# Attention with a fused projection: who copies the o banks, and how the two query casts share a PSUM tile

## Chip, cores, metric

One core of one Trainium2 chip. The metric is the device time of one execution in microseconds (us); for one core that is also the time of the slowest core.

## The reference, cut to what matters

```python
xn = _layernorm(x)                                   # x: 1 x 2048 x 640, bf16
q  = (xn @ wq).reshape(B, Sq, 32, 192)               # 32 heads of 192
p  = softmax(q @ k_cache^T * 192**-0.5)              # 2048 keys for each head
s  = (p @ v_cache) @ wo
g  = silu(swiglu_ffn(xn))                            # 640 -> 1536 -> 640
return x + s * g
```

(The two products are written here as `@`; the reference has them as einsums.) All inputs are bf16. Attention dominates: 32 heads, 2048 queries, 2048 keys.

## The kernel before: the parts that matter

Attention is a stream of 32 x 4 x 8 = 1024 *pairs* (head, block of 512 queries, pair of key tiles). Eight pairs are a *block*; there are 128. At the head of each block (for the first block, inside it) TensorE also computes a query projection of the next head (20 matmuls of 512 columns), so that the queries are there before TensorE needs them; in the last head, two products of the FFN take its place.

```python
def two_products(W, qs):
    ps = ps_st.tile([P, 1024], F32, tag="st2", name="ps")      # the same two buffers as the scores
    ...                                                        # 20 matmuls into two banks
    return ps

def cast_pair(qAB, ps):                                        # PSUM fp32 -> SBUF bf16
    nc.vector.tensor_copy(out=qAB[:, 0, :], in_=ps[:, 0:512])
    nc.scalar.copy(out=qAB[:, 1, :], in_=ps[:, 512:1024])

def emit_scores(h, qb, p):
    st2 = ps_st.tile([P, 1024], F32, tag="st2", name="st2")    # two buffers of two banks each
    ...                                                        # six matmuls
    nc.scalar.activation(out=pT2[:], in_=st2[:], func=ACT.Exp, scale=att_scale)

def values(n):
    ...                                                        # 16 matmuls into obanks[0] and obanks[1]
    if p < NPAIR - 1: return
    nc.scalar.copy(out=osum[:], in_=ov[0])                     # the o copy, once in a block
    nc.vector.tensor_tensor(out=osum[:], in0=osum[:], in1=ov[1], op=ALU.add)

for n, (h, qb, p) in enumerate(stream):
    if p == 0 and n > 0: project(h + 1, qb)                    # two_products, cast_pair, moves by DMA
    scores(n + 2)
    values(n)
    if p == 0 and n > 0: finish_block(n - 1)
    ...                                                        # first head: layernorm of later rows too
```

Terms: a *cast* here is a copy of one half of the projection's result `ps` from PSUM (fp32) to SBUF (bf16); the *o banks* are the two PSUM accumulators of a block's attention output; the *o copy* moves the first of them to `osum`, and the add after it adds the second.

The tag `st2` has two buffers, used in turn: scores of pair n+1, projection, scores n+2, scores n+3. So scores n+3, the *second* scores after a projection, write the buffer that the projection's `ps` held, and must wait until both casts have read it.

## Time and profile before

| | before |
|---|---|
| time | 1989.2 us, median of 3 runs (1988.92 to 1989.59) |
| TensorE (PE) busy | 1958.4 us, 99% |
| ScalarE (ACT) busy | 1260.5 us, 63% |
| VectorE (DVE) busy | 530.7 us, 27% |
| start to start of two projections | 12.933 us in a regular block |

The page of the kernel before: its span, the busy line of section 1 (us, share of the span, number of instructions), and section 4, the chain of work that ended last.

```profile
span 1987.2 us, 60137 instructions
...
PE 1958.4 (99%) x27351; PEld 1395.6 (70%) x27351; DVE 530.7 (27%) x861; ACT 1260.5 (63%) x1405; POOL 319.2 (16%) x572
...
PE 88%; DVE 5%; ACT 4%; issue 1%; DMA 1%; ACTq 0%; DVEq 0%
PE obank L446 30%; PE st L417 27%; PE ps L359 13%; PE ps_s L106 10%; DVE qAB L364 4%; ACT qAB L365 4%; PE st L418 3%; PE ps_f L612 3%; PE ps_gu L586 1%; DMA vt<-in_A_k_cache_dram 1%; PE ps L340 0%; ACT pT L420 0%; DVE stats L295 0%; PE pk L
```

PE seems full, yet the chain goes through both casts (L364 and L365) for 8% of the span. The table of waits of the kernel before (who waited for whom: us in total, times, longest):

```profile
ACT qAB L365 <- DVE qAB L364: 223.5, 126, 1.9
...
PEld L418 <- issue: 35.5, 131, 0.8
```

ScalarE's cast waits for VectorE's cast once in a block (126 times). On the side of PE the loss appears almost only at the weight loads (PEld), and without a culprit ("issue"); the table of PE itself names ScalarE's cast for 1.0 us in 4 waits. One such place in the timeline of the kernel before (start, duration, engine, line, operation, and in brackets the idle time before it and what ended it):

```profile
999.76 0.38 PE L417 MATMUL st<-qAB,KA 64*128 64x512 bf16 x1
...
999.97 0.69 DVE L364 CAST qAB<-ps 128x512 bf16<-128x512 f32 x1
...
1000.40 0.85 PE L446 MATMUL obank<-vt,pT 64*128 64x193 bf16 x16
...
1000.70 0.58 ACT L365 CAST qAB<-ps 128x512 bf16<-128x512 f32 x1 [1.77 <-DVE qAB L364]
...
1001.34 0.37 PE L417 MATMUL st<-qAB,KA 64*128 64x512 bf16 x1
1001.34 0.09 PEld L418 LDWEIGHTS <-KA 64*128 64x128 bf16 x1 [0.26 <-issue]
```

The first scores after the projection start at 999.76, the second at 1001.34, that is 1.58 us later, where the other pairs of a regular block follow one another by 1.314 (by 3.47 where the projection lies between). The values matmuls (L446) are modelled to end at 1001.25, so the PE row shows almost no gap; it is the distance between starts that tells. The second scores start 0.06 us after ScalarE's cast ends at 1001.28.

### The profile page before, as it was taken

The page shows a single profiled execution, that of the slowest core. Times are in us where ns is not written, and L with a number is a line of the kernel's source. Part 1 is how long each engine was busy: PE and PEld are TensorE (multiplying, and loading weights), DVE is VectorE, ACT ScalarE, POOL GpSimd, SP SyncE. Part 2 cuts the span into 40 slices and gives each one's busy share as a digit, 9 for nine tenths or more (in the row PEclk, how much of TensorE's full clock was granted, in tenths as well). Part 3 has the DMA queues.
Part 4 walks back from the last instruction along what each step waited for, and adds up shares of the span by engine and source line. Part 5 has one row for each costly group of instructions (what it writes and reads, how often), then busy time and mean ns, then how long its engine had stood idle before and what let it go on. Part 6 is the DMA issues. An engine that isn't in the chain of part 4 may idle for free.

```text
span 1987.2 us, 60137 instructions
## 1 busy us (share of the span) xinstructions
PE 1958.4 (99%) x27351; PEld 1395.6 (70%) x27351; DVE 530.7 (27%) x861; ACT 1260.5 (63%) x1405; POOL 319.2 (16%) x572
## 2 busy tenths in 40 slices
PE   7999999999999999999999999999999999999999
PEld 5677777777777777777777777777777777577776
DVE  5422222222222222222222222222222223521111
ACT  4677777777777777777777777777777777310000
POOL 3211111111111111111111111111111110000000
PEclk9999999999999999999999999999999999999999
DMA  7423232324332434363433333332323240838873
GB/s 179 90 55 93 58 90 62 97 62 95 67 98 67 98 67 95 67 158 67 98 67 96 65 98 67 80 83 56 92 54 92 59 98 3 232 63 153 153 148 60
DMA packets 362022, 177.96 MB, mean 90 GB/s; under 512 B 305712, under 2 KB 348976, under 8 KB 361760
## 3 DMA queue, kind: packets, MB, share of 16 engines
q1 hardware_dynamic: 334512, 116.21, 27.4%
q0 software_dynamic: 22736, 54.43, 11.1%
q8 instruction: 216, 3.54, 0.7%
q10 hardware_dynamic: 4512, 3.41, 0.6%
q14 instruction: 46, 0.38, 0.1%
HBM read 52.82 MB, written 27.79 MB: 41 GB/s over the span
## 4 chain that ended last, share of the span: by engine, by line
PE 88%; DVE 5%; ACT 4%; issue 1%; DMA 1%; ACTq 0%; DVEq 0%
PE obank L446 30%; PE st L417 27%; PE ps L359 13%; PE ps_s L106 10%; DVE qAB L364 4%; ACT qAB L365 4%; PE st L418 3%; PE ps_f L612 3%; PE ps_gu L586 1%; DMA vt<-in_A_k_cache_dram 1%; PE ps L340 0%; ACT pT L420 0%; DVE stats L295 0%; PE pk L255 0%; PE pst L311 0%
## 5 line engine op out<-in xcount | busy, mean ns | idle before, releaser
L420 ACT ACTIVATE pT<-st 128x1024 bf16<-128x1024 f32 x1024 | 1047.0, 1023 | 209.0 <-PE st L418 203.2
L446 PEld LDWEIGHTS <-pT 64*128 64x128 bf16 x16384 | 745.8, 94 | 208.2 <-issue 0.4
L446 PE MATMUL obank<-vt,pT 64*128 64x193 bf16 x16384 | 867.1, 243 | 0.0
L417 PE MATMUL st<-qAB,KA 64*128 64x512 bf16 x1024 | 384.7, 376 | 13.2 <-ACT qAB L365 1.0
L418 PE MATMUL st<-qAB,KA 64*128 64x512 bf16 x1024 | 386.6, 378 | 0.0
L417 PE MATMUL st<-qC,KC 64*128 64x512 bf16 x1024 | 384.8, 376 | 0.8 <-DVE KC L264 0.8
L417 PE MATMUL st<-qC,KB 64*128 64x512 bf16 x1024 | 384.7, 376 | 0.8 <-DMA qC<-qAB 0.6
L418 PE MATMUL st<-qAB,KB 64*128 64x512 bf16 x1024 | 385.1, 376 | 0.0
L418 PE MATMUL st<-qC,KC 64*128 64x512 bf16 x1024 | 385.1, 376 | 0.0
L456 DVE TENSOR_TENSOR osum<-osum,obank 128x772 f32<-128x772 f32 x128 | 122.6, 958 | 945.8 <-ACT osum L455 945.8
L329 POOL DMA_DIRECT2D qC<-qAB x254 | 133.9, 527 | 1286.5 <-DVE rl_all L462 1265.4
L359 PE MATMUL ps<-xnT,W 64*128 64x512 bf16 x1280 | 299.5, 376 | 0.0
L359 PE MATMUL ps<-xnS,W 64*128 64x512 bf16 x1280 | 293.7, 376 | 0.0
L365 ACT CAST qAB<-ps 128x512 bf16<-128x512 f32 x128 | 74.9, 585 | 227.0 <-DVE qAB L364 223.5
L359 PEld LDWEIGHTS <-W 64*128 64x128 bf16 x2560 | 143.4, 94 | 103.4 <-issue 0.2
L106 PE MATMUL ps_s<-wo_sb,oT 128*128 128x256 bf16 (+3 forms) x1536 | 208.8, 299 | 0.0
L106 PEld LDWEIGHTS <-oT 128*128 128x128 bf16 x1536 | 148.3, 98 | 60.5
L417 PEld LDWEIGHTS <-KC 64*128 64x128 bf16 x1024 | 96.0, 94 | 105.0 <-DVE KC L264 1.1
L463 DVE TENSOR_TENSOR ostage<-osum,rl_all 128x768 bf16<-128x768 f32 x128 | 122.6, 957 | 4.4
L418 PEld LDWEIGHTS <-KA 64*128 64x128 bf16 x1024 | 96.1, 94 | 34.4 <-issue 33.9
L417 PEld LDWEIGHTS <-KA 64*128 64x128 bf16 x1024 | 96.3, 94 | 15.6 <-issue 1.3
L417 PEld LDWEIGHTS <-KB 64*128 64x128 bf16 x1024 | 96.1, 94 | 12.9
(76 smaller groups left out, 1035.2 us busy)
## 6 DMA issues: line engine op xcount, KB each, us to landing
vt<-in_A_v_cache_dram SPq DMA_DIRECT2D x32, 768.0 KB, 6.5
o_scr<-ostage SPq DMA_DIRECT2D x16, 1536.0 KB, 9.3
qC<-qAB POOLq DMA_DIRECT2D x381, 64.0 KB, 2.0
wo_sb<-in_A_wo_dram POOLq DMA_DIRECT2D x1, 7680.0 KB, 37.9
W<-in_A_wq_dram POOLq DMA_DIRECT2D x32, 160.0 KB, 3.3
KC<-KA POOLq DMA_DIRECT2D x31, 128.0 KB, 5.2
KC<-KB POOLq DMA_DIRECT2D x31, 128.0 KB, 5.3
x_all<-in_A_x_dram SPq DMA_DIRECT2D x4, 640.0 KB, 9.7
```

The lines of the kernel that those rows point to most:

```text
L106: nc.tensor.matmul(ps[:, 0:w], lhsT=oT[:, k, :], rhs=wo_sb[:, k, c0:c1], start=(k == 0), stop=(k == OC - 1))
L329: nc.gpsimd.dma_start(out=qC[0:64, half, :], in_=qAB[64:P, half, :])
L359: nc.tensor.matmul(ps[:, r * 512:(r + 1) * 512], lhsT=W[rows, j, :], rhs=xs[rows, j // 2, qs], start=(j == 0), stop=(j == 2 * DC - 1))
L364: nc.vector.tensor_copy(out=qAB[:, 0, :], in_=ps[:, 0:512])
L365: nc.scalar.copy(out=qAB[:, 1, :], in_=ps[:, 512:1024])
L417: nc.tensor.matmul(st2[:, 0:512], lhsT=k0, rhs=q0, start=r == 0, stop=r == 2)
L418: nc.tensor.matmul(st2[:, 512:1024], lhsT=k1, rhs=q1, start=r == 0, stop=r == 2)
L420: nc.scalar.activation(out=pT2[:], in_=st2[:], func=ACT.Exp, scale=att_scale)
L446: nc.tensor.matmul(obanks[r][:, j * 256:j * 256 + DH + 1], lhsT=pT2[r * 64:(r + 1) * 64, t * 512 + j * P:t * 512 + (j + 1) * P], rhs=vt[r ...
L456: nc.vector.tensor_tensor(out=osum[:], in0=osum[:], in1=ov[1], op=ALU.add)
L463: nc.vector.tensor_tensor(out=ostage[:, qb * 4:qb * 4 + 4, hg * DH:(hg + 1) * DH], in0=osum[:, :, 0:DH], in1=rl.unsqueeze(2).to_broadcast( ...
L612: nc.tensor.matmul(ps[:, b * 512:b * 512 + c1 - c0], lhsT=hT[:, fc, i * P:(i + 1) * P], rhs=w2_sb[:, fc, c0:c1], start=(fc == 0), stop=(fc ...
```

## The change

Its intent: take the o copy off ScalarE, give each query half a tile of its own, and let the two casts run at once. The diff, cut to its core:

```diff
-            qtiles[h, qb] = (qp.tile([P, 2, 512], BF16, tag="qAB", name="qAB"), qlp.tile(...))
+            qtiles[h, qb] = ([qp.tile([P, 512], BF16, tag=t, name=t) for t in ("qA", "qB")],
+                             qlp.tile(...))
 ...
     def cast_pair(qAB, ps):
-        nc.vector.tensor_copy(out=qAB[:, 0, :], in_=ps[:, 0:512])
-        nc.scalar.copy(out=qAB[:, 1, :], in_=ps[:, 512:1024])
+        a = nc.vector.tensor_copy(out=qAB[0][:], in_=ps[:, 0:512])
+        b = nc.scalar.copy(out=qAB[1][:], in_=ps[:, 512:1024])
+
+        tc.declare_no_dep(b.ins, a.ins, reason="two banks, two destinations")
 ...                       # every use of qAB[:, half, :] becomes qAB[half][:]
-        nc.scalar.copy(out=osum[:], in_=ov[0])
+        nc.vector.tensor_copy(out=osum[:], in_=ov[0])
```

`declare_no_dep` tells the scheduler that the second cast need not be ordered after the first.

More of the change, by code (lines that the diff above doesn't have):

```diff
@@ L324, in q_tiles @@
         if (h, qb) not in qtiles:
-            qtiles[h, qb] = (qp.tile([P, 2, 512], BF16, tag="qAB", name="qAB"), qlp.tile([P, 2, 512], BF16, tag="qC", name="qC"))
+            qtiles[h, qb] = ([qp.tile([P, 512], BF16, tag=t, name=t) for t in ("qA", "qB")],
+                             qlp.tile([P, 2, 512], BF16, tag="qC", name="qC"))
         return qtiles[h, qb]
     def move_q(qAB, qC, half):
-        nc.gpsimd.dma_start(out=qC[0:64, half, :], in_=qAB[64:P, half, :])
+        nc.gpsimd.dma_start(out=qC[0:64, half, :], in_=qAB[half][64:P, :])
         if half == 0:
-            nc.gpsimd.dma_start(out=qC[64:P, 0, :], in_=qAB[0:64, 0, :])
+            nc.gpsimd.dma_start(out=qC[64:P, 0, :], in_=qAB[0][0:64, :])
     def project0(qb, half):
@@ L342, in project0 @@
         copy = nc.scalar.copy if half else nc.vector.tensor_copy
-        copy(out=qAB[:, half, :], in_=ps[:, 0:512])
+        copy(out=qAB[half][:], in_=ps[:, 0:512])
         if qb > 0:
@@ L375, in ffn_open @@
     def ffn_open(qb):
-        pairs[qb] = qp.tile([P, 2, 512], BF16, tag="qAB", name="qAB")
+        pairs[qb] = [qp.tile([P, 512], BF16, tag=t, name=t) for t in ("qA", "qB")]
         cast_pair(pairs[qb], two_products(wrest["wf"], slice(qb * 512, (qb + 1) * 512)))
@@ L382, in ffn_close @@
         t = hbp.tile([P, 512], BF16, tag="pt", name="pt")
-        nc.scalar.activation(out=t[:], in_=z[:, 0, :], func=ACT.Tanh, scale=0.5)
-        nc.vector.scalar_tensor_tensor(out=t[:], in0=t[:], scalar=1.0, in1=z[:, 0, :], op0=ALU.add, op1=ALU.mult)
+        nc.scalar.activation(out=t[:], in_=z[0][:], func=ACT.Tanh, scale=0.5)
+        nc.vector.scalar_tensor_tensor(out=t[:], in0=t[:], scalar=1.0, in1=z[0][:], op0=ALU.add, op1=ALU.mult)
         nc.vector.scalar_tensor_tensor(out=hT[:, FCP, qb * 512:(qb + 1) * 512], in0=t[:], scalar=0.5,
-                                       in1=z[:, 1, :], op0=ALU.mult, op1=ALU.mult)
+                                       in1=z[1][:], op0=ALU.mult, op1=ALU.mult)
     def swiglu(h, qb):
@@ L391, in swiglu @@
         qs = slice(qb * 512, (qb + 1) * 512)
-        z = qtiles[h, qb][0][0:PGW, 1, :]
+        z = qtiles[h, qb][0][1][0:PGW, :]
         r0 = (m % 2) * PGW
@@ L412, in emit_scores @@
         st2 = ps_st.tile([P, 1024], F32, tag="st2", name="st2")
-        rounds = [(KA[0:64, lo], qAB[0:64, 0, :], KA[64:P, hi], qAB[64:P, 0, :]),
-                  (KB[0:64, lo], qC[0:64, 0, :], KB[64:P, hi], qAB[64:P, 1, :]),
+        rounds = [(KA[0:64, lo], qAB[0][0:64, :], KA[64:P, hi], qAB[0][64:P, :]),
+                  (KB[0:64, lo], qC[0:64, 0, :], KB[64:P, hi], qAB[1][64:P, :]),
                   (KC[0:64, lo], qC[0:64, 1, :], KC[64:P, lo], qC[64:P, 0, :])]
```

## The prediction

> **What bounds it now.** TensorE: the page gives PE 1958.4 us busy of 1987.2 (99%), ScalarE 63%, VectorE 27%. Attention runs to about 1697 us as 128 blocks of eight pairs (scores, exponential, values), each with one projection at its head. In the timeline around 1000 us the score matmuls of two pairs start 1.314 us apart (3.47 with the projection between). One interval per block differs: the scores of the second pair after the projection start 1.579 us after the ones before (999.76 to 1001.34), 0.265 us late. Over the matmul starts of the whole trace this happens in 121 of 128 blocks; block to block is 12.933 us where 12.67 would do. Pipelined matmuls drain over the gap, so PE shows only 13.2 us idle at this line; the table of waits shows it at the weight loads, 35.5 us in 131 waits, put down to "issue".
>
> **Its cause.** These scores reuse the PSUM buffer of the projection's `ps`, which both casts must leave. VectorE's cast runs 999.97 to 1000.66 and only then ScalarE's, 1000.70 to 1001.28, though ScalarE had been idle since 998.93 (table of waits: 223.5 us in 126 waits for VectorE's cast). PE resumes at 1001.34. The chain of waits runs through the casts (4% + 4%), although PE was held for only 0.265 us of each 1.3.
>
> **What the change does.**
> - Casts side by side, in tiles of their own: `ps` is free after the longer one, at about 1000.67 instead of 1001.28. PE wants it at 999.76 + 1.314 = 1001.07. So the wait goes whole, with 0.35 us to spare; what the casts gain beyond 0.265 us is worth nothing.
> - o copy from ScalarE (0.797 us) to VectorE. Estimate 0.96 us: VectorE's 512-element fp32 cast takes 0.692, its 772-element add from PSUM 0.958. The Trainium skill ("VectorE: DVE Perf Modes", "Why PSUM operands drop a tier") agrees: 1x for fp32 from PSUM. ScalarE's copy starts at 1011.06, behind an exponential; VectorE is idle and can start when the values end, near 1010.75. Copy and add then end near 1012.7 against 1012.85 now, before VectorE's cast (1012.91) and the next values matmuls (1013.34). VectorE rises from 531 to about 655 us, ScalarE falls by 102: neither bounds, so this half alone is worth about 0.
> - Both casts read `ps` at once, from two banks. "PSUM — Partial Sum Buffer", Specifications, says that this runs at full bandwidth without a bank collision; the trace before doesn't show it.
> - Nothing after 1697 us changes; no DMA, no matmul is added.
>
> **Sum.** 126 x 0.265 = 33 us; the first head's irregular blocks may give or take 1 us.
>
> **Prediction: 1956.5 us** (1.6% faster), range 1952 to 1963. Chances: faster by over 2% (below 1949.4) 0.03; within 2% 0.95; slower 0.02.
>
> **What would show each step.** Regular blocks of 12.67 us, the second interval 1.31; PE's weight-load waits on "issue" down from 35 us to a few; ScalarE's wait for VectorE's cast gone (223 us to about 0), the two casts starting within 0.1 us; o copy on VectorE near 0.96 us; the casts gone from the chain of waits, PE at 95% or more of it; PE's busy total hardly moved.
>
> **What would make it wrong.** The o copy takes over 1.2 us and pushes VectorE's cast back (over 1.5: the values wait for o banks); casts slow each other; ScalarE's cast still waits for VectorE's; the exponential after the cast, now earlier, uncovers another 0.1-0.2 us wait.

## The result, and the profile after

1957.45 us, median of 4 runs (1956.91 to 1957.77), against 1989.21 us of before in the same rounds. The ratio is 0.984 (95% interval 0.9823 to 0.9857), 1.6% faster; it is inside the range that was predicted. Ratios here are the mean time of one kernel's fast runs over that of the other's in the same rounds, so not quite the ratio of the medians.

The page of the changed kernel, the same lines:

```profile
span 1955.9 us, 59887 instructions
...
PE 1937.5 (99%) x27351; PEld 1390.2 (71%) x27351; DVE 654.1 (33%) x989; ACT 1184.2 (61%) x1277; POOL 319.2 (16%) x572
...
PE 98%; DVE 1%; DMA 1%; ACT 0%; issue 0%; DVEq 0%; ACTq 0%
PE obank L449 35%; PE st L420 31%; PE ps L360 14%; PE ps_s L106 11%; PE st L421 3%; PE ps_f L615 3%; PE ps_gu L589 1%; DMA vt<-in_A_k_cache_dram 1%; PE ps L341 0%; ACT pT L423 0%; DVE stats L295 0%; PE pst L311 0%; PE pk L255 0%; DMA qC<-qA
```

The casts are gone from the chain. Note what the busy line does *not* tell: PE is at 99% before and after, and its busy time fell by 20.9 us although it executes the same matmuls. The table of waits of the changed kernel:

```profile
ACT qB L366 <- PE ps L360: 222.0, 128, 1.7
...
PE obank L449 <- DVE osum L459: 1.6, 2, 0.8
...
PEld L421 <- issue: 2.3, 4, 0.8
```

ScalarE idles just as long before its cast (222 us, before 223.5), but now it waits for the projection's end, not for VectorE: the total of a wait says little, its end says all. PE's unexplained weight-load waits before the scores fell from 35.5 us to 2.3. One line is new: the values waited twice for VectorE's add, 0.8 us each; we come back to it. The timeline of the changed kernel at a regular block:

```profile
993.38 0.96 DVE L458 COPY osum<-obank 128x772 f32<-128x772 f32 x1 [4.91 <-PE obank L449]
...
994.45 0.96 DVE L459 TENSOR_TENSOR osum<-osum,obank 128x772 f32<-128x772 f32 x1
...
995.35 0.38 PE L420 MATMUL st<-qA,KA 64*128 64x512 bf16 x1
...
995.56 0.69 DVE L365 CAST qA<-ps 128x512 bf16<-128x512 f32 x1 [0.15 <-PE ps L360]
995.56 0.38 PE L420 MATMUL st<-qC,KB 64*128 64x512 bf16 x1
995.56 0.58 ACT L366 CAST qB<-ps 128x512 bf16<-128x512 f32 x1 [1.74 <-PE ps L360]
...
996.66 0.38 PE L420 MATMUL st<-qA,KA 64*128 64x512 bf16 x1
```

Both casts start at 995.56, and the second scores follow the first by 1.31 us. Copy and add on VectorE end 0.15 us before its cast could start anyway.

Where the time came from, counted on the starts of the projections in the whole trace: from the fifth projection to the last, the changed kernel needs 32.5 us less in 123 blocks (12.672 against 12.933 us each); from the first scores to the fifth projection, in the first head, it needs 0.8 us *more* (70.47 against 69.63 us; a second trace of the changed kernel has 70.07). The prediction's 33 us is there; so is a small loss that it had not counted.

### The profile page after: what moved, and what is told of

Read it like the earlier page. It is cut to its first block, busy times and chain, and to the rows that moved or that the text cites. A ratio compares the mean times of both kernels' runs of the same rounds, so it can differ in the third digit from the quotient of the medians.

```text
span 1955.9 us, 59887 instructions
## 1 busy us (share of the span) xinstructions
PE 1937.5 (99%) x27351; PEld 1390.2 (71%) x27351; DVE 654.1 (33%) x989; ACT 1184.2 (61%) x1277; POOL 319.2 (16%) x572
## 4 chain that ended last, share of the span: by engine, by line
PE 98%; DVE 1%; DMA 1%; ACT 0%; issue 0%; DVEq 0%; ACTq 0%
PE obank L449 35%; PE st L420 31%; PE ps L360 14%; PE ps_s L106 11%; PE st L421 3%; PE ps_f L615 3%; PE ps_gu L589 1%; DMA vt<-in_A_k_cache_dram 1%; PE ps L341 0%; ACT pT L423 0%; DVE stats L295 0%; PE pst L311 0%; PE pk L255 0%; DMA qC<-qA 0%; ACT xnT L314 0%
## 5 line engine op out<-in xcount | busy, mean ns | idle before, releaser
L420 PE MATMUL st<-qA,KA 64*128 64x512 bf16 x1024 | 385.4, 376 | 1.6 <-ACT pT L423 0.9
L421 PE MATMUL st<-qA,KA 64*128 64x512 bf16 x1024 | 385.6, 377 | 0.0
L421 PE MATMUL st<-qB,KB 64*128 64x512 bf16 x1024 | 385.5, 376 | 0.0
L458 DVE COPY osum<-obank 128x772 f32<-128x772 f32 x128 | 123.2, 962 | 784.0 <-PE obank L449 784.0
L330 POOL DMA_DIRECT2D qC<-qA x127 | 67.1, 528 | 1239.4 <-DVE rl_all L465 1235.9
L366 ACT CAST qB<-ps 128x512 bf16<-128x512 f32 x128 | 74.9, 585 | 222.0 <-PE ps L360 222.0
L401 DVE SCALAR_TENSOR_TENSOR hT<-pt,qB 64x512 bf16<-64x512 bf16 x64 | 43.8, 684 | 204.2 <-ACT pt L400 204.2
L420 PEld LDWEIGHTS <-KA 64*128 64x128 bf16 x1024 | 96.4, 94 | 15.8 <-issue 1.3
```

Source lines behind the costliest of these rows:

```text
L330: nc.gpsimd.dma_start(out=qC[0:64, half, :], in_=qAB[half][64:P, :])
L366: b = nc.scalar.copy(out=qAB[1][:], in_=ps[:, 512:1024])
L420: nc.tensor.matmul(st2[:, 0:512], lhsT=k0, rhs=q0, start=r == 0, stop=r == 2)
L421: nc.tensor.matmul(st2[:, 512:1024], lhsT=k1, rhs=q1, start=r == 0, stop=r == 2)
L458: nc.vector.tensor_copy(out=osum[:], in_=ov[0])
```

## The experiments

My theory was: the only gain is that `ps` comes free before TensorE wants it; the o copy on VectorE is worth nothing in a regular block and costs a little in the first head. Rivals: the relief of ScalarE is part of the gain; the tiles of their own are what frees the casts; two engines must work at once. Eleven kernels were run, all correct. They fell on three chips; the runs of before beside them had medians of 1989.09 to 1989.25 us, so the chips agree within 0.2 us.

### The changed kernel again

No edit; a yardstick on the chip of the next three.

> The changed kernel once more, as the yardstick for the runs beside it. Every theory: 1957.4 us within 1 us; before 1989.2.

Measured: 1957.01 us (1956.83 to 1957.37), ratio 0.9838.

### The casts alone

```diff
 # from the changed kernel
-        nc.vector.tensor_copy(out=osum[:], in_=ov[0])
+        nc.scalar.copy(out=osum[:], in_=ov[0])
```

> The casts of the change alone; the o copy stays on ScalarE. My theory (only the release of the ps buffer matters; the o copy on VectorE is worth 0 in regular blocks and costs 2 x 0.58 us in the first head, where VectorE is busy with layernorm and values wait for its add): regular blocks 12.67 us, total 1956.3 us, about 1.1 below the changed kernel, and no wait of the values for VectorE's add in the first head. Rival (the relief of ScalarE by 102 us is part of the gain): clearly slower than the changed kernel, 1965 to 1985.

Measured: 1955.18 us (1954.71 to 1955.26), ratio 0.9828: 1.83 us *below* the changed kernel. The rival (relief of ScalarE) falls: ScalarE is at 1273.9 us busy (before the change 1260.5), and nothing is lost. The waits of the values for VectorE's add are gone. The direction was right; the size, 1.8 us, is more than the 1.1 expected.

### The o copy alone

```diff
 # from the kernel before
-        nc.scalar.copy(out=osum[:], in_=ov[0])
+        nc.vector.tensor_copy(out=osum[:], in_=ov[0])
```

> The o copy on VectorE alone; casts one after the other as before. My theory: blocks stay at 12.93 us, the first head loses about 1.1 us more, total 1990.3 us. Rival (relief of ScalarE): 1960 to 1982.

Measured: 1991.21 us (1990.99 to 1991.44), ratio 1.001 (0.9996 to 1.0023). By itself this half gains nothing: regular blocks stay at 12.933 us. The median is 2.0 us above the before of the same rounds, and the slowest of its 9 runs of before (1989.53) is below the fastest here.

### The o copy back on ScalarE in the first head only

```diff
 # from the changed kernel
-        nc.vector.tensor_copy(out=osum[:], in_=ov[0])
+        (nc.scalar.copy if h == 0 else nc.vector.tensor_copy)(out=osum[:], in_=ov[0])
```

> The changed kernel, but in the first head (four blocks) the o copy is done by ScalarE. My theory: the two waits of the values for VectorE's add (0.78 us each, 0.58 us of block time each) go, 1956.3 us, about 1.1 below the changed kernel and equal to the casts alone. Rival (those waits are hidden by the other delays of the first head): 1957.4.

Measured: 1955.45 us (1954.86 to 1955.85), ratio 0.9829. Four blocks of 128 bring back 1.6 of the 1.8 us. So the loss lies in the first head, and in the other 31 heads either engine may do the copy.

What happens there. The timeline of the changed kernel in its first head, where VectorE also computes the layernorm statistics of later rows (L295, L296, L299):

```profile
44.47 0.87 DVE L295 BATCH_NORM_STATS2 stats<-x_all 128x6 f32<-128x320 bf16 x2
...
45.70 0.95 DVE L458 COPY osum<-obank 128x772 f32<-128x772 f32 x1
...
46.08 0.38 PE L420 MATMUL st<-qA,KA 64*128 64x512 bf16 x1
...
46.76 0.96 DVE L459 TENSOR_TENSOR osum<-osum,obank 128x772 f32<-128x772 f32 x1
...
47.63 0.68 DVE L365 CAST qA<-ps 128x512 bf16<-128x512 f32 x1
47.77 0.82 PE L449 MATMUL obank<-vt,pT 64*128 64x193 bf16 x15 [0.78 <-DVE osum L459]
...
48.37 0.39 PE L420 MATMUL st<-qA,KA 64*128 64x512 bf16 x1
```

Copy, add and cast stand in one queue behind the statistics. The values wait 0.78 us for the second o bank, and the second scores start 2.29 us after the first. With the o copy on ScalarE and the casts free (the kernel of "The declaration alone" below, same place):

```profile
43.91 0.87 DVE L295 BATCH_NORM_STATS2 stats<-x_all 128x6 f32<-128x320 bf16 x2
44.08 0.79 ACT L456 COPY osum<-obank 128x772 f32<-128x772 f32 x1
...
45.14 0.96 DVE L457 TENSOR_TENSOR osum<-osum,obank 128x772 f32<-128x772 f32 x1
...
45.52 0.38 PE L418 MATMUL st<-qAB,KA 64*128 64x512 bf16 x1
...
46.83 0.38 PE L418 MATMUL st<-qAB,KA 64*128 64x512 bf16 x1
```

ScalarE copies *while* VectorE is at the statistics, and the second scores follow after 1.31 us. The interval between first and second scores in the two blocks of the first head where this happens, read from the starts in the traces:

| kernel | 2nd block | 3rd block |
|---|---|---|
| before | 1.86 us | 1.95 us |
| the o copy alone | 2.91 us | 3.00 us |
| changed | 2.30 us | 2.40 us |
| the casts alone | 1.31 us | 1.34 us |
| o copy on ScalarE in the first head | 1.31 us | 1.33 us |

From the casts alone to the changed kernel: 0.99 + 1.06 = 2.05 us, where 1.83 us were measured. The expected 1.1 us was too small because I took the changed kernel's first head against that of before, which itself still paid 0.5 to 0.6 us in each of these blocks for the casts in a row.

### The tiles without the declaration

```diff
 # from the changed kernel
         a = nc.vector.tensor_copy(out=qAB[0][:], in_=ps[:, 0:512])
         b = nc.scalar.copy(out=qAB[1][:], in_=ps[:, 512:1024])
-        tc.declare_no_dep(b.ins, a.ins, reason="two banks, two destinations")
```

> The changed kernel without the declaration that the two casts are independent. The two compiled programs differ in nothing but the waits of ScalarE's cast (VectorE in place of PE) and one wait of the scores after it. My theory (both casts read the tile ps, and the scheduler orders them by that alone): casts one after the other again, blocks 12.93 us, 1990 us (1989.2 plus 1.1 of the first head). Rival (the shared destination tile was what ordered them): 1957.4.

Measured: 1991.05 us (1990.49 to 1991.73), ratio 1.0011: the whole gain is gone. The timeline of this kernel:

```profile
1001.67 0.69 DVE L365 CAST qA<-ps 128x512 bf16<-128x512 f32 x1 [0.15 <-PE ps L360]
...
1002.40 0.59 ACT L366 CAST qB<-ps 128x512 bf16<-128x512 f32 x1 [2.47 <-DVE qA L365]
...
1003.04 0.37 PE L420 MATMUL st<-qA,KA 64*128 64x512 bf16 x1
```

Two destinations do not help. The only tile that the two casts still share is `ps`, which both only *read*, each in a bank of its own; so, by elimination, it is this sharing by which the scheduler orders them. (That two separate tiles for the halves of `ps` would free the casts as well was not run. In the first head the changed kernel has undeclared readers of one `ps` with different destinations too, and they also follow one another: ScalarE's cast at 20.94 for 0.59 us, VectorE's at 21.56; but those read the same bank.)

### The declaration without the tiles

```diff
 # from "the o copy alone": the shared tile stays
-        nc.vector.tensor_copy(out=qAB[:, 0, :], in_=ps[:, 0:512])
-        nc.scalar.copy(out=qAB[:, 1, :], in_=ps[:, 512:1024])
+        a = nc.vector.tensor_copy(out=qAB[:, 0, :], in_=ps[:, 0:512])
+        b = nc.scalar.copy(out=qAB[:, 1, :], in_=ps[:, 512:1024])
+        tc.declare_no_dep(b.ins, a.ins, reason="two banks, two destinations")
```

> The declaration and the o copy on VectorE, with the one shared destination tile of before. My theory: the casts start together, blocks 12.67 us, 1957.4 us within 1. Rival (the shared destination tile orders them, by its own dependency): 1990.

Measured: 1957.62 us (1957.14 to 1957.72), ratio 0.9841, the same as the changed kernel. The two halves of one destination tile do not order the casts. The tiles of their own are worth nothing measurable beside the declaration.

### Both casts by ScalarE; both casts by VectorE

```diff
 # from the changed kernel; the other one has nc.vector.tensor_copy twice
-        a = nc.vector.tensor_copy(out=qAB[0][:], in_=ps[:, 0:512])
-        b = nc.scalar.copy(out=qAB[1][:], in_=ps[:, 512:1024])
-        tc.declare_no_dep(...)
+        nc.scalar.copy(out=qAB[0][:], in_=ps[:, 0:512])
+        nc.scalar.copy(out=qAB[1][:], in_=ps[:, 512:1024])
```

> Both casts by ScalarE, one after the other. By the trace ScalarE starts its next instruction 0.48 us after a cast's start, so the second cast ends 0.48 + 0.585 = 1.065 us after ps is ready, when PE wants the buffer at about 1.10 less some 0.05 for the signal. My theory (only the time of release counts, against PE's own 1.1 us): a delay of 0 to 0.04 us per block, 1957 to 1963 us. Rival (the gain needs two engines at work at once): 1989 or so.

Measured: 1959.78 us (1959.72 to 1960.13), ratio 0.9853.

> Both casts by VectorE, one after the other. VectorE's next instruction starts 0.61 us after a cast's start, so release comes 0.61 + 0.69 = 1.30 us after ps is ready, some 0.25 us later than PE wants it. My theory: blocks 12.92 us, 1988 us within 4 (VectorE's later work also moves). Rival (two casts in a row on one engine are enough, as no signal goes between engines): under 1965.

Measured: 1988.53 us (1988.23 to 1989.19), ratio 0.9997.

The timeline of the kernel with both casts on ScalarE:

```profile
983.56 0.38 PE L418 MATMUL st<-qA,KA 64*128 64x512 bf16 x1
...
983.78 0.58 ACT L365 CAST qA<-ps 128x512 bf16<-128x512 f32 x1 [1.74 <-PE ps L360]
...
984.26 0.59 ACT L366 CAST qB<-ps 128x512 bf16<-128x512 f32 x1
...
984.90 0.37 PE L418 MATMUL st<-qA,KA 64*128 64x512 bf16 x1
```

No two engines work at once here, and 91% of the gain is kept (29.4 us of the 32.2 us of the yardstick). ScalarE starts its second cast 0.48 us after the first, so both are done 1.07 us after `ps` was ready; on VectorE the same takes 1.29 us, and nothing is left. Simultaneity is not what pays. Being done in time is.

### The release half a microsecond late

```diff
 # from "the casts alone"
-        b = nc.scalar.copy(out=qAB[1][:], in_=ps[:, 512:1024])
+        for k in range(3):                       # two copies go to spare tiles that nobody reads
+            dst = qAB[1] if k == 2 else hbp.tile([P, 512], BF16, tag=f"dm{k}", name=f"dm{k}")
+            b = nc.scalar.copy(out=dst[:], in_=ps[:, 512:1024])
+            tc.declare_no_dep(b.ins, a.ins, ...)
```

> The casts of the change alone, with ScalarE made to cast its half three times (two copies are thrown away), side by side with VectorE. By the trace each further cast adds 0.48 us: ps is released 0.96 + 0.585 + 0.05 = 1.60 us after it is ready, when PE wants it after 1.10. My theory: each block 0.50 us longer, 13.17 us, total 1955.2 + 126 x 0.50 = 2018 us within 4. Rival (each added ScalarE time counts in full): 2 x 0.48 per block, 2076 us.

Measured: 2020.45 us (2020.17 to 2020.92), ratio 1.0158. Blocks take 13.185 us. The timeline of this kernel (`dm` are the spare tiles):

```profile
1004.53 0.69 DVE L365 CAST qA<-ps 128x512 bf16<-128x512 f32 x1
1004.53 1.07 ACT L368 CAST dm<-ps 128x512 bf16<-128x512 f32 x2 [1.05 <-PE ps L360]
1005.49 0.61 ACT L368 CAST qB<-ps 128x512 bf16<-128x512 f32 x1
1006.14 0.37 PE L421 MATMUL st<-qA,KA 64*128 64x512 bf16 x1 [0.34 <-ACT qB L368]
```

The casts end 1.57 us after `ps` was ready. Only now does the table of PE name the right culprit in every block (`ACT qB L368`, 42.9 us in 127 waits; before the change 1.0 us in 4). With this run there are five points of one curve. (The end of the last cast is counted from the start of the first; the block time is the median of the starts of regular blocks; the delay is that over 12.672 us.)

| kernel | last cast ends after | block | delay of a block |
|---|---|---|---|
| changed: side by side | 0.69 us | 12.672 us | 0 |
| both on ScalarE | 1.07 us | 12.696 us | 0.024 us |
| both on VectorE | 1.29 us | 12.914 us | 0.242 us |
| before: VectorE, then ScalarE | 1.31 us | 12.933 us | 0.261 us |
| ScalarE three times | 1.57 us | 13.185 us | 0.513 us |

The delay is the end of the last cast less 1.05 us (1.05, 1.05, 1.05 and 1.06 in the four rows with a delay), and nothing below that. The trace of before gives the same limit: PE wants the buffer 1.10 us after `ps` is ready (999.76 + 1.314 - 999.97), and the scores start 0.05 to 0.06 us after the last cast ends. The casts of the change end 0.36 us inside this limit.

### The o copy twice

```diff
 # from the changed kernel
+        dup = osp.tile([P, 4, DH + 1], F32, tag="dup", name="dup")     # nobody reads it
+        nc.vector.tensor_copy(out=dup[:], in_=ov[0])
         nc.vector.tensor_copy(out=osum[:], in_=ov[0])
```

> The changed kernel with the o copy done twice by VectorE (one is thrown away), to find how near it is to harm. Copy, copy and add, 0.96 to 1.07 us each, then end near 983.70 in the time of the trace after, where the values want the second o bank at 983.33 and VectorE's cast could start at 982.89. My theory: blocks 0.40 to 0.50 us longer, 2007 to 2021 us. Rival (VectorE is 33% busy, so 123 us more of it hide): 1957 to 1960.

Measured: 1996.45 us (1995.99 to 1996.6), ratio 1.0037; blocks of 12.960 us. Both were wrong: the rival, since 0.96 us of work on an engine that is 33% busy cost 0.29 us in each block, and my size, 0.40 to 0.50. The timeline of this kernel:

```profile
1003.06 0.96 DVE L459 COPY dup<-obank 128x772 f32<-128x772 f32 x1 [4.87 <-PE obank L449]
...
1003.94 0.95 DVE L460 COPY osum<-obank 128x772 f32<-128x772 f32 x1
...
1004.99 0.96 DVE L461 TENSOR_TENSOR osum<-osum,obank 128x772 f32<-128x772 f32 x1
...
1005.67 1.16 PE L449 MATMUL obank<-vt,pT 64*128 64x193 bf16 x16
1005.87 0.68 DVE L365 CAST qA<-ps 128x512 bf16<-128x512 f32 x1
...
1006.01 0.59 PEld L449 LDWEIGHTS <-pT 64*128 64x128 bf16 x14 [0.41 <-issue]
...
1006.61 0.39 PE L420 MATMUL st<-qA,KA 64*128 64x512 bf16 x1
```

I had added whole durations. The second copy starts 0.88 us after the first, not 0.96, as neither needs the other's result; the add, which needs the second copy's, starts 1.05 us after it. The add then ends at 1005.95, and VectorE's cast ends at 1006.55, just before the second scores start at 1006.61. Here two waits fall together: the values matmuls are stretched to 1.16 us (0.85 in the changed kernel), and `ps` comes late by about as much. The traces tell which one ends last. The cast ends 1.29 us after `ps` is ready (median of the blocks), as with both casts on VectorE, where that alone cost 0.242 us in a block; here the block lost 0.288. And in every regular block only one of the 16 values matmuls starts before the add ends, the second starts 0.05 us after it, and from there to the scores PE takes 0.605 us (0.62 in the next pair), so nothing more is lost to `ps`. The wait for the o bank sets the loss, and `ps` alone would have cost nearly as much. That is read from traces; no run parts the two.

### The declaration alone

The experiments point to a kernel smaller than the change: before, plus the declaration.

```diff
 # from the kernel before
-        nc.vector.tensor_copy(out=qAB[:, 0, :], in_=ps[:, 0:512])
-        nc.scalar.copy(out=qAB[:, 1, :], in_=ps[:, 512:1024])
+        a = nc.vector.tensor_copy(out=qAB[:, 0, :], in_=ps[:, 0:512])
+        b = nc.scalar.copy(out=qAB[:, 1, :], in_=ps[:, 512:1024])
+        tc.declare_no_dep(b.ins, a.ins, reason="two banks, two halves")
```

> The kernel before plus the declaration and nothing else: shared destination tile, o copy on ScalarE. My theory (the declaration is the whole gain, the o copy on VectorE a loss in the first head): 1955.2 us, the same as the casts of the change alone, about 1.9 below the changed kernel. Rival (the tiles of their own or the o copy are needed beside it): 1957 or more.

Measured: 1954.95 us (1954.79 to 1955.91), ratio 0.983 (0.9817 to 0.9843). It is as fast as the casts alone and about 2 us faster than the changed kernel; each of the five runs is below every run of the changed kernel (lowest 1956.83).

## Why the prediction was right, and what was mis-sized

- **What bounds: right.** The late second scores were the loss. Removing that wait gave 32.5 us in 123 regular blocks by the trace, where 126 x 0.265 = 33 us was predicted for all.
- **Its cause: right, and now shown.** The curve above ties the delay to the end of the last cast with one constant. The predicted "0.35 us to spare" measures 0.36. "What the casts gain beyond 0.265 us is worth nothing" is shown from the other side: casts that take 1.07 us instead of 0.69 lose only 0.024 us in a block.
- **"Casts side by side, in tiles of their own": half of it was idle.** The prediction did not part the tiles from the declaration. The declaration does everything (1954.95 us alone); the tiles without it do nothing (1991.05 us).
- **"This half alone is worth about 0" (the o copy): right in regular blocks, mis-sized in the first head.** The step that failed is "VectorE is idle and can start when the values end". In two blocks of the first head VectorE is at the layernorm statistics, the copy queues behind them, and values and casts wait: this costs 1.8 us by the changed kernel against the casts alone, and 2.0 us by the o copy alone against before. The prediction had given the first head 1 us either way. The number still came out 1.0 us off (1957.45 for 1956.5), well inside the range: the loss is small beside 32 us, and the free casts gained about 1.5 us in the first head (from the first scores to the fifth projection, which opens the second head, 68.11 us instead of 69.63, in the trace of the declaration alone), where 126 x 0.265 had counted about 0.8 for its three blocks. That the two errors offset each other in part is luck.
- **The duration of the o copy: right.** 962 ns measured, 0.96 us estimated. (ScalarE's busy total, however, fell by 76 us, from 1260.5 to 1184.2, where 102 was predicted; why is not shown, and ScalarE bounds nothing here.) The Trainium skill ("VectorE: DVE Perf Modes", "Why PSUM operands drop a tier") says that fp32 from PSUM runs at 1x; the trace agrees: (962 - 692) ns for 772 - 512 elements is 1.04 ns each.
- **Two readers of `ps` at once: right.** "PSUM — Partial Sum Buffer", "Specifications (TRN2)", says that ScalarE and VectorE can access PSUM at the same time at full bandwidth, as long as no bank collides. The trace after agrees: the casts take 691 and 585 ns side by side in the mean, and took 692 and 585 one after the other.
- **"PE's busy total hardly moved": wrong.** It fell by 20.9 us. Part of every wait had been counted as busy, as the modelled ends of the matmuls in front reach over it (to 1001.25 in the block above, where the scores were wanted at 1001.07). The Trainium skill ("Perfetto Trace Analysis", "Identifying the Most-Contended Engine") warns that matmul busy share is not a good measure of how close PE is to its peak, because pipelined instructions look smaller in the trace. The warning holds here, but the error goes the other way: PE looked busier than it was, and 99% before hid the 32 us.

What is left open: whether two tiles for `ps` would do as well as the declaration; and the last 0.3 us between the casts alone and the o copy on ScalarE in the first head. Their ranges overlap, and one interval of the first head (third to fourth projection) differs by 0.5 us between their traces; it differs by 0.4 us between two traces of the same changed kernel too.

## What to carry to other kernels

Look for an instruction that always starts late by the same amount and compare start to start, since a pipelined TensorE at 99% busy can hide 1.6% of the time; then ask which buffer it reuses and when its *last* reader ends. Two readers of different banks of one tile may be serialized by the scheduler alone; one declaration of independence can be worth more than moving work between engines. And before moving work to an engine that is "27% busy", look at the stretches in which it is not idle: an average gives no slack where queue order decides.

## What the Trainium skill lacked or had wrong

- "VectorE: DVE Perf Modes", the table of op costs under the errata: its PSUM row, (120 + elements) cycles at 0.96 GHz, gives 929 ns for the 772-element o copy and 658 ns for the 512-element cast; the runs show 962 and 692 from start to end, and 0.88 and 0.61 us from start to start of instructions that do not wait, so the row fits neither. The form with 151 cycles that the same page gives for adds fits both (961 and 691).
- "Perfetto Trace Analysis", "Identifying the Most-Contended Engine", offers the busy share of the weight loads, their summed time over the window, as a better gauge of TensorE. It is not one here: the loads, 27351 of about 94 ns in each of these kernels, overlap, and their sum is 130% of the span before and 132% after, a change that only repeats the shorter span. The profile's own figure, which counts overlapping loads once, does no better: the same changed kernel shows 71% in one trace and 77% in another (1957.77 and 1957.37 us), and the declaration alone 88%.
- No page that I looked up says that the scheduler orders two engines that only read one tile, in different banks. That order cost 34 us here (1989.1 against 1954.95 us), and the destination tiles had no part in it.
